# Attention scores of a head pair in two row halves of the array, in six bursts instead of eleven steps

## The chip, the cores and the metric

The kernel runs on one core of one Trainium2 chip. A core has a matmul engine (PE, whose weight loads PEld overlap its matmuls), a vector engine (DVE), a scalar engine (ACT), a general engine (POOL) and a queue engine that issues DMAs (SP). Matmuls write PSUM, eight banks of 512 floats in each of 128 partitions; DVE and ACT read them there, POOL cannot. Each engine works its instructions in order and waits on semaphores that the others raise. The metric is device time in microseconds (us), the median of a few runs. For the kernel before it is 1928.92 us (three runs, 1925.21 to 1930.3).

## The reference

Input x has 2048 tokens of width 576. What is computed, cut to what matters:

```
h   = layernorm(x) * (1 + ca) + sa
q, k, v = h @ wq, h @ wk, h @ wv         # 32 heads of width 18, 4 segments of 512 tokens
p   = softmax(q k^T / sqrt(18) + causal mask)     # inside a segment
a   = g * (phi(q) @ M) / (phi(q) @ z) + (1 - g) * (p @ v)    # M, z: sums over earlier segments
x   = x + ga * (a @ wo)
h   = layernorm(x) * (1 + cb) + sb
out = x + gb * ((silu(h @ w_gate) * (h @ w_up)) @ w_down)
```

## The kernel before, in words

Three stages follow one another. **Projections** (to about 256 us): x is normalized, transposed and multiplied by the projection weights, each product as three matmuls of high and low halves; q, k and v go to DRAM (qD, kD, vD). **Attention** (about 256 to 613 us). **Feed-forward** (the rest).

Attention works in 32 *units*: segment s = 0 to 3 by group q = 0 to 7 of four heads. A unit has two passes over its scores. The *first pass* (`p1_step`, L177) multiplies queries by keys (matmul L187) into PSUM bank s1, and DVE takes each row's maximum (L192, a custom reduction followed by a read of its accumulator). After the last one POOL splits the negated maxima into high and low parts (L197 to L200), PE transposes them (`mt_a`, L206), ACT copies them to mr (L210) and issues their store to DRAM buffer mD (L211); `load_m` (L173, issued by SP) reads them back into two extra rows of the query stack. The *second pass* (`p2_step`, L578) multiplies again (L589), now with those two rows against rows of ones in the key stack, so that the maxima are subtracted by the matmul itself; ACT takes the exponential out of bank s2 into Pt (L592), POOL zeroes the masked corner (L596). Then `av_step` (L600) multiplies by the values: four heads' matmuls of 32 output columns each (L609), one group for each of four key blocks j; these are full float32 and appear as two instructions each, where the score matmuls are rounded float32 and appear as one. `ev_step` copies av out (ACT, L621), `comb_a` transposes it (PE, L630), `comb_b` scales it by the row sums (DVE) and adds it to the memory part (POOL).

The operands of the scores are *stacks*. For a pair of heads the key stack holds 108 rows: head e=0 in rows 0 to 53, head e=1 in rows 54 to 107 (18 dimensions, three times for the high, high and low parts), and the ones in rows 108 and 109. The query stack has four slots, one for each head, and in each slot the rows of the other head of the pair are zero (`new_stack`, L122, writes the zeros by memset). So each head's score matmul uses 108 or 110 of 128 rows, of which 54 carry data. There are four sets of stacks (b = u % 4); `load_stack` (L164) fills one with four DMAs.

In the main loop (L1284 to L1297) a pass over unit u loads the stacks of unit u+3, runs the second pass of unit u and the first pass of unit u+2, and the rest of the neighbours' work. The order is written out by hand (`manual_schedule`): both passes are generators of eleven steps (four steps each for 512 and 384 columns, two for 256, one for 128), one step of each is taken in turn, and after step k come the *events* that the string PAT[..][k] lists. PAT has four rows: q below 4 or not, u even or odd. Both passes rotate through two banks (S1B, S2B = 2), one bank a step.

Events that matter here: V0 to V3 the value matmuls of block j (V2 and V3 belong to the unit before); E, c, d its copy-out, transpose and combination; m and n the transpose of the maxima, and their copy, store and reload; M0 to M3 quarters of an output projection (`wo_m`, PE, L707) and X its addition (DVE); R, S, T the transpose, copy and low part of its input; l, p, x the statistics (DVE), power (POOL) and normalization (`ln_c`, ACT, L739) of the following layernorm; g three ACT activations on queries of the next segment (`phi_q2`, L756 to L758), in the first five units of segments 0 to 2; A0, A1, B0, B1, C, D, G the memory product for the next segment (`num_a` on PE, L778, `num_b` on ACT, L787), in the last four units of segments 0 to 2; P, Q, q, Y the preparation of the output weights, in segment 0; f a DMA.

The first passes of units 0 and 1 (`early`, L256) run among the projections, where a scheduler orders instructions; `p1_unit` (L213) is a generator there.

Of the kernel before, what the change touches and what calls it, by code (L numbers as in the profile page):

```python
# [15 lines left out]
P = 128  # L16
S = 2048
# [44 lines left out]
PAT = (["", "V2", "V3 E m D", "M0", "n M1 Q G", "c", "M2 d", "V0 g", "h A0 q M3 R S X", "T Y Z B0", "A1 P V1 z B1 f C"],  # L62
       ["V2 D", "l M0 Q", "V3 m E", "M1", "G p n A0 B0 M2", "", "M3 X A1 q c x d B1", "f", "V0 g", "", "C V1 Y h P"],
       ["", "V2", "V3 m E", "M0", "D G M1 c n", "", "Q V0 d g R", "h", "M2 q M3 A0 S B0 X", "Z Y", "P f z V1 A1 T B1 C"],
       ["", "V2 m", "l D n p G M0", "V3", "M1 E M2 A0", "", "M3 x c", "B0", "V0 d Q", "A1 g", "q X V1 Y B1 h P C f"])
# [9 lines left out]
def block(ctx: ExitStack, tc: tile.TileContext, x, wqk, wv, wo, beta, wgu, wd, c, w_mod, out):  # L75
# [46 lines left out]
    def new_stack(b, stk):  # L122
        qst[b] = stk.tile([P, 4, L], F32R, tag=f"qs{b}", name=f"qs{b}")
        kst[b] = stk.tile([P, 2, L], F32R, tag=f"ks{b}", name=f"ks{b}")
        nc.vector.memset(f32(qst[b][:, 0:2]), 0.0)
        nc.gpsimd.memset(f32(qst[b][:, 2:4]), 0.0)
        nc.sync.dma_start(f32(kst[b][108:110]).rearrange("p a (b c) -> p (a b) c", c=P),
                          ones[0:2, :].unsqueeze(1).to_broadcast([2, 8, P]))
# [35 lines left out]
    def load_stack(u, b):  # L164
        s, q = units[u]
        for e in range(2):
            v = [d[s].rearrange("f z t -> (f z) t").rearrange("(Q a e r) t -> Q e r a t", Q=8, a=2, e=2)[q, e]
                 for d in (kD, qD)]
            r = slice(54 * e, 54 * e + 54)
            nc.sync.dma_start(f32(kst[b][r]), v[0])  # L170
            nc.sync.dma_start(f32(qst[b][r, e:4:2, :]), v[1])

    def load_m(u, b):  # L173
        nc.sync.dma_start(f32(qst[b][108:110]).rearrange("p a t -> p (a t)"),
                          m_dram(u).rearrange("(a b) t -> a (b t)", a=2))

    def p1_step(u, b, i, ps, jp, jb):  # L177
        if i == 3:
            mcol[u] = (mwk.tile([P, 4, 4], F32, tag="mx", name="mx"),
                       mwk.tile([P, 2, 4, 4], F32R, tag="mc", name="mc"))  # L180
        mx, mc = mcol[u]
        n = 128 * (i + 1)
        per = L // n if n <= 256 else 1
        for h0 in range(0, 4, per):
            bank = ps.tile([P, L], F32, tag="s1", name="s1", bufs=S1B)
            for h in range(h0, h0 + per):
                nc.tensor.matmul(bank[:, n * (h - h0):n * (h - h0) + n],  # L187
                                 lhsT=qst[b][0:108, h, 128 * i:128 * i + 128],
                                 rhs=kst[b][0:108, h // 2, 0:n], start=True, stop=True)
            for h in range(h0, h0 + per):  # L190
                junk = jp.tile([P, L], BF16, tag="junk", name="junk", bufs=jb)
                nc.vector.tensor_tensor_reduce(junk[:, :n], bank[:, n * (h - h0):n * (h - h0) + n], tri[:, L - n:],  # L192
                                               1.0, -3e38, op0=ALU.add, op1=ALU.max, accum_out=mx[:, h, i:i + 1])
            if h0 + per < 4:
                yield
# [5 lines left out]
        yield  # L201
# [11 lines left out]
    def p1_unit(u, b, ps, tag, bufs, jp, jb):  # L213
        for i in range(4):
            yield from p1_step(u, b, 3 - i, ps, jp, jb)
# [355 lines left out]
    def p1_seq(u):  # L571
        if NE <= u < NU:
            for i in range(4):
                yield from p1_step(u, u % NB, 3 - i, ps, wk, 4)

    Pt, av = {}, {}

    def p2_step(u, j):  # L578
        if u >= NU:
            return  # L580
        n = L - 128 * j
        per = L // n if n <= 256 else 1
        pt = pp_.tile([P, 4, n], F32, tag=f"P{j}", name="Pt", bufs=1)
        Pt[u, j] = pt
        for h in range(0, 4, per):
            bank = ps.tile([P, L], F32, tag="s2", name="s2", bufs=S2B)
            for g in range(h, h + per, 2):
# [966 lines left out]
```

## Time and profile before

| what | value |
|---|---|
| median of three runs | 1928.92 us |
| the profiled execution, its own time | 1926.12 us |
| its span (first to last instruction) | 1924.3 us |
| granted clock of PE, mean over the span | 0.996 |
| stage with attention units | about 256 to 613 us |

The profile shows one execution. A row of a group or timeline reads: source line, engine, operation, output <- input, shapes; then busy time or start and duration in us, and in brackets the idle time before it with what ended it. In a merged timeline row the time is that from the first start to the last end. Matmuls overlap, since the next one fills the array while the last one drains: the duration shown for one (about 0.4 us) is longer than the distance to the next (about 0.235 us for 512 columns). In the chain of waits each piece is what the one before it did not cover, so there the distance is shown.

### The profile page before, as it was taken

The page shows a single profiled execution, that of the slowest core. Times are in us where ns is not written, and L with a number is a line of the kernel's source. Part 1 is how long each engine was busy: PE and PEld are TensorE (multiplying, and loading weights), DVE is VectorE, ACT ScalarE, POOL GpSimd, SP SyncE. Part 2 cuts the span into 40 slices and gives each one's busy share as a digit, 9 for nine tenths or more (in the row PEclk, how much of TensorE's full clock was granted, in tenths as well). Part 3 has the DMA queues.
Part 4 walks back from the last instruction along what each step waited for, and adds up shares of the span by engine and source line. Part 5 has one row for each costly group of instructions (what it writes and reads, how often), then busy time and mean ns, then how long its engine had stood idle before and what let it go on. Part 6 is the DMA issues. An engine that isn't in the chain of part 4 may idle for free.

```text
span 1924.3 us, 30622 instructions
## 1 busy us (share of the span) xinstructions
PE 1874.0 (97%) x10927; PEld 1562.5 (81%) x10927; DVE 1512.8 (79%) x3267; ACT 929.8 (48%) x2036; POOL 581.0 (30%) x772
## 2 busy tenths in 40 slices
PE   7999999999999799999999999999999999999999
PEld 4888865676766678888888888888888888888888
DVE  6575257878786888898898888776888888888887
ACT  2222257767666444445445444443544444454542
POOL 5222235555544554545444545410000000000000
PEclk9999999999999899999999999999999999999999
DMA  7777565444443555454454554478333233333331
GB/s 209 251 230 245 199 200 150 124 147 145 138 127 117 172 199 175 155 191 151 159 186 154 163 168 145 137 246 267 101 106 113 79 122 101 122 101 97 106 108 60
DMA packets 173543, 296.63 MB, mean 154 GB/s; under 512 B 25104, under 2 KB 101776, under 8 KB 171920
## 3 DMA queue, kind: packets, MB, share of 16 engines
q1 hardware_dynamic: 143280, 237.09, 39.4%
q10 hardware_dynamic: 30112, 57.60, 8.6%
q8 instruction: 86, 1.41, 0.3%
q14 instruction: 65, 0.53, 0.1%
HBM read 185.29 MB, written 109.31 MB: 153 GB/s over the span
## 4 chain that ended last, share of the span: by engine, by line
PE 88%; DMA 5%; DVE 4%; POOL 1%; issue 1%; ACT 1%; SPq 0%; ACTq 0%; POOLq 0%; DVEq 0%
PE A L1136 23%; PE pd L1257 13%; PE C L1136 12%; PE pd L1240 9%; PE B L1136 6%; PE s L589 4%; PE av L609 4%; PE pp L101 4%; PE s L187 4%; PE pv L101 3%; PE pw L707 2%; DMA y<-yD 1%; DMA mD<-mr 1%; PE pn L778 1%; DVE y L938 1%
## 5 line engine op out<-in xcount | busy, mean ns | idle before, releaser
L1136 PE MATMUL A<-y,wh 128*128 128x512 f32 x1152 | 406.8, 394 | 4.3 <-ACT B L1182 1.8
L192 DVE CUSTOM_DVE_ANT_0 junk<-s,tri 128x256 bf16<-128x256 f32 (+3 forms) x512 | 228.6, 487 | 75.6 <-PE s L187 67.6
L1101 DVE TENSOR_TENSOR wl<-O,wh 128x256 fp32r<-128x256 f32 x504 | 261.7, 525 | 4.2 <-ACT wh L1100 3.5
L1136 PEld LDWEIGHTS A<-y,wh 128*128 128x128 f32 x1152 | 217.2, 189 | 49.0 <-ACT B L1182 2.5
L592 ACT ACTIVATE Pt<-s 128x512 f32<-128x512 f32 (+1 forms) x352 | 186.6, 559 | 86.2 <-PE s L589 71.6
L1136 PE MATMUL A<-y,wl 128*128 128x512 f32 x576 | 227.2, 394 | 0.0
L1091 POOL TENSOR_TENSOR O<-O 128x384 f32<-128x384 f32 x144 | 163.3, 1146 | 179.1 <-DMA O<-in_wgu_dram 76.0
L1245 DVE TENSOR_TENSOR acc<-acc,pd 128x576 f32<-128x576 f32 x216 | 162.4, 752 | 58.6 <-PE pd L1240 51.7
L1136 PE MATMUL C<-y,wh 128*128 128x512 f32 x576 | 202.6, 392 | 1.0 <-DVE cu L1159 1.0
L1100 ACT CAST wh<-O 128x256 fp32r<-128x256 f32 x504 | 196.4, 405 | 1.9 <-POOL dr__8754 L1119 1.2
L1257 PE MATMUL pd<-dh,ah 128*128 128x288 f32 x640 | 189.1, 295 | 0.1
L1257 PE MATMUL pd<-dh,al 128*128 128x288 f32 x640 | 189.1, 295 | 0.0
L1257 PE MATMUL pd<-dl,ah 128*128 128x288 f32 x640 | 188.9, 295 | 0.0
L1261 DVE TENSOR_TENSOR acc<-acc,pd 128x576 f32<-128x576 f32 x156 | 116.9, 749 | 89.0 <-PE pd L1257 88.9
L1200 ACT CAST ah<-sg 128x512 fp32r<-128x512 f32 x192 | 119.1, 620 | 82.7 <-DVE sg L1160 77.6
L589 PE MATMUL s<-qs,ks 110*128 110x512 f32 (+2 forms) x384 | 149.2, 405 | 6.6 <-DMA qs<-mD 4.8
L187 PE MATMUL s<-ks,qs 108*128 108x256 f32 (+3 forms) x512 | 140.7, 326 | 2.9 <-DMA ks<-kD 1.4
L1201 DVE TENSOR_TENSOR al<-sg,ah 128x512 fp32r<-128x512 f32 x192 | 135.2, 704 | 8.8 <-ACT ah L1200 8.4
L1240 PE MATMUL pd<-dh,ah 128*128 128x288 f32 x448 | 133.0, 297 | 0.0
L1240 PE MATMUL pd<-dh,al 128*128 128x288 f32 x448 | 132.5, 296 | 0.0
L1240 PE MATMUL pd<-dl,ah 128*128 128x288 f32 x448 | 132.3, 295 | 0.0
L1257 PEld LDWEIGHTS pd<-dl,ah 128*128 128x128 f32 x640 | 120.5, 188 | 7.1
(349 smaller groups left out, 4394.4 us busy)
## 6 DMA issues: line engine op xcount, KB each, us to landing
O<-in_wgu_dram SPq DMA_DIRECT2D x36, 768.0 KB
oD<-O ACTq DMA_DIRECT2D x36, 512.0 KB
O<-oD SPq DMA_DIRECT2D x36, 512.0 KB
ks<-kD SPq DMA_DIRECT2D x68, 216.0 KB
qs<-qD SPq DMA_DIRECT2D x68, 216.0 KB
O<-in_wgu_dram SPq DMA_DIRECT2D x36, 384.0 KB
rD<-wr ACTq DMA_DIRECT2D x36, 336.0 KB
wr<-rD SPq DMA_DIRECT2D x35, 336.0 KB
```

Of the source, the lines that this page charges most:

```text
L187: nc.tensor.matmul(bank[:, n * (h - h0):n * (h - h0) + n], lhsT=qst[b][0:108, h, 128 * i:128 * i + 128], rhs=kst[b][0:108, h // 2, 0:n], s ...
L192: nc.vector.tensor_tensor_reduce(junk[:, :n], bank[:, n * (h - h0):n * (h - h0) + n], tri[:, L - n:], 1.0, -3e38, op0=ALU.add, op1=ALU.max ...
L589: nc.tensor.matmul(bank[:, n * (g - h):n * (g - h + w)].rearrange("p (a b) -> p a b", a=w), lhsT=kst[u % NB][0:110, g // 2, 128 * j:128 * ...
L592: nc.scalar.activation(pt[:, h:h + per, :n], bank[:, :n * per].rearrange("p (a b) -> p a b", a=per), AF.Exp, scale=SCALE)
L1091: nc.gpsimd.tensor_tensor(o[:, d], o[:, a], o[:, b], op=op)
L1100: nc.scalar.copy(wh, o)
L1101: later.append(lambda: nc.vector.tensor_tensor(wl, o, f32(wh), op=ALU.subtract))
L1136: nc.tensor.matmul(bank, lhsT=a, rhs=b, start=(first and n == 0), stop=(n == 6), skip_group_check=not first)
L1201: later.append(lambda: nc.vector.tensor_tensor(al, src, f32(ah), op=ALU.subtract))
L1240: nc.tensor.matmul(pd[:, i, :288], lhsT=a[:, tk], rhs=w, start=(k == 0), stop=(k == 2))
L1245: nc.vector.tensor_tensor(o, o, pd[:, :, :288], op=ALU.add)
L1257: nc.tensor.matmul(pd[:, i, :288], lhsT=a[:, tk], rhs=w, start=(k == 0), stop=(k == 5))
```

## The change

The two heads of a pair no longer share one column of rows. Key stack and query stack hold head e=0 in rows 0 to 53 and head e=1 in rows 64 to 117; each half has its own two rows of ones (keys) and of maxima (queries) behind its 54. The query stack shrinks from four slots to two, and the zeros with their memsets are gone. Each score matmul reads only the 54 or 56 rows of its half, and the built program gives it a tile of 64 rows by 128 columns at row 0 or 64. The ones are written by two DMAs a stack instead of one, the maxima are read back by two instead of one; the stack loads keep their count and size.

The eleven steps become six bursts (BI gives the row block, BA the pairs): two with 512 columns, two with 384, one with both pairs of 256, one with both pairs of 128. A burst takes both s1 banks, one for each half, and issues the first-pass matmuls in the order e=0, e=1, then its reductions; the second pass does the same with both s2 banks and its exponentials, now two instructions in every burst. The second pass no longer joins two heads in one matmul for the narrow blocks: 16 matmuls a unit instead of 12, and 12 exponentials instead of 11. The events are regrouped into six strings in each row of PAT.

```diff
-PAT = (["", "V2", "V3 E m D", "M0", "n M1 Q G", "c", "M2 d", "V0 g", "h A0 q M3 R S X", "T Y Z B0", "A1 P V1 z B1 f C"],
-       ["V2 D", "l M0 Q", "V3 m E", "M1", "G p n A0 B0 M2", "", "M3 X A1 q c x d B1", "f", "V0 g", "", "C V1 Y h P"],
-       ["", "V2", "V3 m E", "M0", "D G M1 c n", "", "Q V0 d g R", "h", "M2 q M3 A0 S B0 X", "Z Y", "P f z V1 A1 T B1 C"],
-       ["", "V2 m", "l D n p G M0", "V3", "M1 E M2 A0", "", "M3 x c", "B0", "V0 d Q", "A1 g", "q X V1 Y B1 h P C f"])
+PAT = (["V2 M0", "V3 E m D M1", "n Q G c M2", "d V0 g", "h M3 A0 q R S X Y Z B0", "T A1 P V1 z B1 f C"],
+       ["V2 D l M0 Q", "V3 m E M1", "n G p A0 c M2", "d V0 g B0 q x", "M3 A1 X B1 f", "C V1 Y h P"],
+       ["V2 M0", "V3 m E M1", "n D G c M2", "Q V0 d g R", "h M3 q A0 S X Z Y B0", "P f z V1 A1 T B1 C"],
+       ["V2 m l M0", "V3 E n D p G M1", "A0 c M2 x", "B0 V0 d Q", "M3 A1 g X q", "V1 Y B1 h P C f"])
+BI = (3, 3, 2, 2, 1, 0)
+BA = ((0,), (1,), (0,), (1,), (0, 1), (0, 1))
...
-        qst[b] = stk.tile([P, 4, L], F32R, tag=f"qs{b}", name=f"qs{b}")
+        qst[b] = stk.tile([P, 2, L], F32R, tag=f"qs{b}", name=f"qs{b}")
...
-        nc.vector.memset(f32(qst[b][:, 0:2]), 0.0)
-        nc.gpsimd.memset(f32(qst[b][:, 2:4]), 0.0)
-        nc.sync.dma_start(f32(kst[b][108:110]).rearrange("p a (b c) -> p (a b) c", c=P),
-                          ones[0:2, :].unsqueeze(1).to_broadcast([2, 8, P]))
+        for e in range(2):
+            nc.sync.dma_start(f32(kst[b][64 * e + 54:64 * e + 56]).rearrange("p a (b c) -> p (a b) c", c=P),
+                              ones[0:2, :].unsqueeze(1).to_broadcast([2, 8, P]))
...
     def load_m(u, b):
-        nc.sync.dma_start(f32(qst[b][108:110]).rearrange("p a t -> p (a t)"),
-                          m_dram(u).rearrange("(a b) t -> a (b t)", a=2))
+        v = m_dram(u).rearrange("(c a e i) t -> e c a (i t)", c=2, a=2, e=2)
+        for e in range(2):
+            nc.sync.dma_start(f32(qst[b][64 * e + 54:64 * e + 56]), v[e])
...
+        banks = [ps.tile([P, L], F32, tag="s1", name="s1", bufs=S1B) for _ in range(2)]
+        for x, a in enumerate(BA[t]):
+            for e in range(2):
+                r = slice(64 * e, 64 * e + 54)
+                nc.tensor.matmul(banks[e][:, n * x:n * x + n], lhsT=qst[b][r, a, 128 * i:128 * i + 128],
+                                 rhs=kst[b][r, a, 0:n], start=True, stop=True)
+        for e in range(2):
+            for x, a in enumerate(BA[t]):
...
+                nc.vector.tensor_tensor_reduce(junk[:, :n], banks[e][:, n * x:n * x + n], tri[:, L - n:],
...
     def p1_unit(u, b, ps, tag, bufs, jp, jb):
-        for i in range(4):
-            yield from p1_step(u, b, 3 - i, ps, jp, jb)
+        for t in range(6):
+            p1_burst(u, b, t, ps, jp, jb)
+            yield
+            yield
...
+    def p2_burst(u, t):
...
+        banks = [ps.tile([P, L], F32, tag="s2", name="s2", bufs=S2B) for _ in range(2)]
+        w = len(BA[t])
+        for x, a in enumerate(BA[t]):
+            for e in range(2):
+                r = slice(64 * e, 64 * e + 56)
+                nc.tensor.matmul(banks[e][:, n * x:n * x + n], lhsT=kst[u % NB][r, a, 128 * j:128 * j + 128],
+                                 rhs=qst[u % NB][r, a, 128 * j:L], start=True, stop=True)
+        for e in range(2):
+            h = 2 * BA[t][0] + e
+            nc.scalar.activation(pt[:, h:h + 2 * w - 1:2, :n], banks[e][:, :n * w].rearrange("p (a b) -> p a b", a=w),
                                  AF.Exp, scale=SCALE)
...
-            for k in range(11):
-                next(ga, None)
-                next(gb, None)
-                for ev in PAT[q // 4 * 2 + u % 2][k].split():
+            for t in range(6):
+                if NE <= u + 2 < NU:
+                    p1_burst(u + 2, (u + 2) % NB, t, ps, wk, 4)
+                if u < NU:
+                    p2_burst(u, t)
+                for ev in PAT[q // 4 * 2 + u % 2][t].split():
                     event(ev, u)
```

## The prediction

> **What bounds the kernel now.** I read the page first (span and busy shares), then busy time in windows cut at attention units, then the chain of waits inside one unit, then single rows for prices.
>
> ```profile
> span 1924.3 us, 30622 instructions
> PE 1874.0 (97%) x10927; PEld 1562.5 (81%) x10927; DVE 1512.8 (79%) x3267; ACT 929.8 (48%) x2036; POOL 581.0 (30%) x772
> ```
>
> The matmul engine is the pace-maker on average, but the change touches only the attention stage (about 256 to 613 us) and two early units inside the projections, so an average decides nothing. Five units, by window (PE, weight loads, DVE, ACT, POOL):
>
> ```profile
> core 0: us, PE busy (x) PEld busy (x) DVE busy (x) ACT busy (x) POOL busy (x), PEclk, DMA share, GB/s
> 311.00:322.47 11.47, 10.28 (x78) 6.77 (x77) 10.14 (x45) 7.84 (x17) 8.44 (x17) 1.00 0.52 141
> 446.24:457.14 10.90, 10.90 (x83) 7.35 (x79) 10.04 (x44) 8.68 (x18) 4.18 (x10) 1.00 0.49 151
> 457.14:468.28 11.14, 11.14 (x88) 7.70 (x84) 8.46 (x34) 8.73 (x18) 6.71 (x12) 1.00 0.45 135
> 504.13:516.44 12.31, 12.31 (x97) 8.94 (x94) 9.56 (x43) 7.28 (x15) 6.44 (x16) 1.00 0.55 150
> 550.86:562.00 11.14, 11.14 (x88) 7.70 (x84) 8.46 (x34) 7.06 (x14) 3.65 (x9) 1.00 0.42 132
> ```
>
> They are units 5, 17, 18, 22 and 26. PE is never idle in the last four, but DVE needs 8.5 to 10.0 us and ACT 7.1 to 8.7 us of each: whatever PE gives up, at most 1 to 3 us can be kept, and less where a queue is lumpy. The chain inside unit 22 (start, us, work):
>
> ```profile
> 504.87 0.23 PE s L589
> 505.10 0.23 PE s L187
> 505.33 0.57 PE av L609 x8
> 505.90 0.43 PE s L589
> ...
> 506.55 0.36 PE av L609 x8
> ...
> 509.50 0.18 PE s L187
> ...
> 510.02 1.00 PE av L609 x8
> ...
> 512.19 0.24 PE s L187 x2
> 514.09 0.24 PE s L589
> 514.57 0.24 PE s L589 x2
> 514.81 0.40 PE s L187 x4
> ```
>
> A score matmul costs 0.235 us for 512 columns, 0.18 for 384, 0.12 for 256, 0.10 for 128. One unit's first pass (L187: four of each width) is 2.53 us; the second (L589: four of 512, four of 384, two paired to 512, two paired to 256) is 2.37. Together 4.9 us of 12.3.
>
> **Part 1: pairs in two 64-row halves.** The same columns are streamed, but heads e=0 and e=1 stand in different row halves and write different banks. No row of this profile has two row halves in work. The nearest is av, four 32-column tiles: 8 instructions in 0.36 us for 128 columns and 1.00 for 512, so 0.21 us per further 128 columns for eight, where one score matmul takes 0.06 per 128 columns. Eight one after another could not; the four tiles run side by side. So a pair costs between 1.0 and 2.0 single matmuls; I take 1.0. Scores become 1.26 + 1.26 = 2.5 us, PE saves 2.4 us a unit; at 2.0 it saves nothing, and the four 128-wide second-pass matmuls that replace two 256-wide ones cost 4 x 0.10 - 2 x 0.12 = 0.16 more.
>
> The Trainium skill, page "TensorE: Matmul & The Clock Gate", section "Part 3: Packing small matmuls — row/col tiling", gives 3.07 times for four row tiles; scaled to two (an estimate from that figure) a pair costs 1.3 singles, the saving falls to 1.7 us a unit, and a unit bound by PE alone would gain 0.8 instead of 1.5 us. No run here shows it yet.
>
> **Part 2: array modes.** Every burst sets the array to 64-row tiles while av uses 32 columns and all else the whole array. In the built order of the matmuls the changes of tile shape grow from 257 to 432 within attention (5.5 more a unit) and from 34 to 79 before it. The price stands in the rows: after av, a 512-column score matmul takes 0.43 instead of 0.24, so 0.19 to leave; av's 0.36 less its 0.21 per 128 columns leaves 0.15 to enter. A 64-row tile already occurs among the projections, in the last transposes of a key block:
>
> ```profile
> 38.39 0.40 PE L101 MATMUL pp<-hr,wqkl 128*128 128x512 f32 x1
> 38.62 0.60 PE L429 MATMUL ptk<-ident,pf 128*128 128x128 f32 x4
> 39.30 0.40 PE L101 MATMUL pp<-hh,wqkl 128*128 128x512 f32 x1
> 53.19 0.40 PE L101 MATMUL pp<-hr,wqkl 128*128 128x512 f32 x1
> 53.52 0.46 PE L429 MATMUL ptk<-ident,pf 64*128 64x64 f32 x4
> 54.24 0.39 PE L101 MATMUL pp<-hh,wqkl 128*128 128x512 f32 x1
> ```
>
> From the projection before to the second one after: 0.91 us with whole-array transposes, 1.05 with 64-row ones although those are 0.14 shorter: 0.28 for in and out. So a switch is 0.14 to 0.19; I take 0.17. Attention pays 5.5 x 0.17 = 0.9 us a unit.
>
> The skill's page "TensorEngine Tiling (Array Packing)", section "Tiling Modes", says that changing the mode drains the engine, which speaks against short bursts; these rows agree and give the price, 0.17 us.
>
> PE alone would so gain 2.4 - 0.9 = 1.5 us a unit.
>
> **Part 3: what the other engines allow.** A burst fills both banks of each pass, so the next burst needs two reductions and two exponentials done. Before, each of eleven steps took one bank of two.
>
> ```profile
> 452.86 0.87 ACT L739 ACTIVATE xh<-xr,nb,rs 128x576 f32<-128x576 f32 x1
> 453.63 0.96 ACT L592 ACTIVATE Pt<-s 128x384 f32<-128x384 f32 x2
> 454.48 0.63 ACT L756 ACTIVATE qe<-qf 128x512 f32<-128x512 f32 x1
> 455.14 0.63 ACT L757 ACTIVATE qe<-qe 128x512 f32<-128x512 f32 x1
> 455.68 0.61 ACT L758 ACTIVATE qf<-qf 128x512 f32<-128x512 f32 x1
> 456.20 1.06 ACT L592 ACTIVATE Pt<-s 128x512 f32<-128x512 f32 x2
> ```
>
> Odd units of segments 1 and 2 with q below 4 (9, 11, 17, 19): events g and x, two steps apart before with exponentials between, now both stand behind burst 4. I walk PE: four bursts 0.17 + two pairs (0.64, 0.64, 0.53, 0.53), av 0.57 and 0.36, the small transposes and seven projection matmuls about 2.4, 0.35 wait because ln_a now sits on DVE behind burst 1: burst 4 ends at 6.1. Its two exponentials end at 7.05, g (1.8 from start to end) at 8.85, x at 9.7, burst 5's two exponentials (1.06) at 10.8. Burst 6's second pass waits until then (PE was ready near 9.5); with 0.2 for it and about 0.8 for av the unit ends at 11.9, against 10.9 for unit 17. The four together +3.3 us. Their even neighbours have only g there: 10.75 against 11.14 (unit 18); the four of them -1.3.
>
> Full units (segments 1 and 2, q from 4; like unit 22) have pn and pw between the bursts: PE stays the bound, -1.0 after the DVE wait of the odd ones; six of them, -0.6 for unit 20 and 0 for unit 12 (next paragraph): -6.6. Segment 3 (like unit 26) loses its cover: burst 6 waits for burst 5's four reductions (DVE's L192 is 228.6 us over 32 units, 7.1 each, first row below), ending near 10.5: -0.5 a unit, -3.7 for units 24 to 30.
>
> ```profile
> L192 DVE CUSTOM_DVE_ANT_0 junk<-s,tri 128x256 bf16<-128x256 f32 (+3 forms) x512 | 228.6, 487 | 75.6 <-PE s L187 67.6
> 282.32 4.51 DMA mD<-mr
> 280.43 0.34 SPq L171 DMA_DIRECT2D qs<-qD  x1
> 286.84 0.23 SPq L174 DMA_DIRECT2D qs<-mD  x1
> 320.30 2.04 DMA qs<-mD
> ```
>
> Segment 0, and units 11, 12 and 19, wait for the row maxima's way through DRAM: written at 282.32 behind stack loads issued until 280.43, landed only when SP issues the read at 286.84, 2.04 more to land, and the next unit starts. Those loads keep their size, so the units keep their length. The maxima's copy now stands behind six exponentials instead of five, and there are two reads instead of one (0.23 of SP): +0.2 to +0.8 where the loads did not already set it. Segment 0 together +1.4.
>
> Attention: 3.3 - 1.3 - 6.6 - 3.7 + 1.4 = -6.9 us.
>
> **Part 4: outside.** The scheduler spreads the first two units' bursts among projections: 45 more switches, 7.6 us, less some 1.5 for pairs that stay together.
>
> ```profile
> by line: PE pp L101 33.3%; PE pv L101 20.3%; DVE junk L192 5.1%; issue 4.8%; DMA wml<-in_w_mod_dram 4.7%; PE s L187 3.7%; DVE macc L303 3.2%; DVE x L232 3.1%; PE pt L237 2.9%; PE pc L310 2.3%; POOL rs L228 2.0%; DVE pk L433 1.7%; PE ptk L42
> 245.85 1.49 SPq L127 DMA_DIRECT2D ks<-ones  x2
> 250.43 0.76 SPq L171 DMA_DIRECT2D qs<-qD  x1
> 250.43 8.83 DMA qs<-qD
> ```
>
> The first row is the chain from 85 to 160 us, about 63% PE, so 6.1 x 0.63 = +4 (bounds 0 and 7.6). At the stage's start the ones take four issues instead of two ahead of unit 2's loads, whose landing (last row) held unit 0: +1.4 (bounds 0 and 1.5). The removed zeroing (eight memsets) delayed no PE work there; I give it 0.
>
> **Sum**: -6.9 + 4 + 1.4 = -1.5 us. The profiled execution took 1926.12 us (1.8 outside its span), 2.8 below the median of 1928.92; so 1924.6 on its scale, 1927 on the median's.
>
> **Rivals.** (a) *PE keeps what it saves.* For it: PE is 100% busy in four of the five units. Then 24 units (all but the eight held by the maxima) gain 1.5: 1928.9 - 36 + 5.4 = 1898. Against it: DVE already 10.0 in unit 17. (b) *ACT's lump spreads.* All 15 units that carry g, not just four, wait for burst 5's exponentials. It decides once ACT has over about 2.2 us (av 1.00, a burst 0.5, pw 0.7) between the exponentials of bursts 4 and 5; g alone is 1.8. Eleven more at +1.1: 1939. (c) *The change doesn't do what it says*: halves do not overlap. Each unit then pays 0.9 + 0.2: 32 x 1.1 = 35, half of it hidden in the eight held units, so 31, + 5 + 1.4: 1966. For it: each second half waits on a semaphore of its own.
>
> **How the numbers follow.** My forecast, an even trade, 0.45, own range 1918 to 1937; (a) 0.20; (b) 0.20; (c) 0.15. Change smaller than 0.3% (5.8 us) can't be told from none. Of the even trade 0.12 falls faster, 0.20 within, 0.13 slower. Faster 0.12 + 0.20 = 0.32, same 0.20, slower 0.13 + 0.20 + 0.15 = 0.48. The range 1905 to 1958 leaves out half of (a) and two thirds of (c). It includes a pair a third of the way to no overlap (1.3 singles: 0.7 us less on some 13 units that PE bounds, +9) and switches at 0.14 or 0.19 (5 us either way).
>
> **What would show it.** Scores of a pair starting together, at most 0.02 us apart; matmuls after a burst 0.15 to 0.2 late; units 17 and 18 near 11.9 and 10.75, unit 22 near 11.3; the weight-load queue waiting for ACT ahead of burst 6; the projections some 4 us longer. I am wrong if PE still has no idle time in odd units, or if second halves start only when first halves end.

## The result, and the profile after

The change makes the kernel slower: 1975.68 us against 1927.47 (medians of four runs each), ratio 1.0249 with a 95% interval of 1.0231 to 1.0266. The forecast was 1927 in a range of 1905 to 1958; it is wrong.

The span grew by 48.5 us, from 1924.3 to 1972.8. I cut it at the first exponential of a unit (in the trace every 11th row of `Pt<-s` on ACT before, every 12th after):

| part | before | after | difference | forecast |
|---|---|---|---|---|
| start to unit 0's first exponential (projections, start of the stage) | 257.5 | 272.3 | +14.8 | +5.4 |
| from there to unit 31's | 346.3 | 377.3 | +31.0 | -6.9 |
| the rest | 1320.5 | 1323.2 | +2.7 | 0 |

The page of after, its head and the row of the granted clock in 40 slices of 49.3 us:

```profile
span 1972.8 us, 30927 instructions
PE 1904.1 (97%) x11055; PEld 1535.7 (78%) x11055; DVE 1506.8 (76%) x3263; ACT 926.8 (47%) x2068; POOL 573.5 (29%) x768
PEclk9999976999999999999999999999999999999999
```

PE's busy time rose by 30 us although it has less to stream, and the clock shows 0.7 and 0.6 in the slices where attention starts. In windows (columns: busy us and instructions of each engine, granted clock, DMA), cut at the start of attention and behind units 5 and 30, after reads

```profile
240.00:271.50 31.50, 27.01 (x165) 24.29 (x163) 3.91 (x7) 5.54 (x12) 2.48 (x4) 0.97 0.81 263
271.50:349.00 77.50, 71.35 (x414) 34.03 (x416) 49.45 (x211) 49.35 (x106) 35.55 (x56) 0.66 0.43 123
349.00:649.00 300.00, 283.64 (x2179) 162.25 (x2177) 225.14 (x933) 194.93 (x425) 141.50 (x295) 0.96 0.42 121
```

and before, for the same units as the last two,

```profile
256.50:323.00 66.50, 58.82 (x392) 34.61 (x392) 51.55 (x213) 49.67 (x102) 36.90 (x60) 1.00 0.56 164
323.00:603.00 280.00, 279.08 (x2076) 193.42 (x2074) 222.66 (x931) 197.81 (x400) 139.76 (x291) 1.00 0.43 129
```

The clock takes two values, 1.0 and 0.5, in stretches of 3.41 us or a multiple. Summed, 109 us of after ran at half clock up to 740 us (20 before unit 0, 76 in attention, 14 behind it) against 14 of before. The largest wait of PE's two queues in attention (us in all, times, longest), in after and then in before, shows the other change: the weight loads of a burst now wait for DVE's reductions, where those of a step waited, for less, for ACT's exponentials.

```profile
PEld s L190 <- DVE mx L195: 70.0, 152, 1.3
```

```profile
PEld s L589 <- ACT Pt L592: 39.9, 66, 1.4
```

So three suspects: G, the granted clock, set off by thinner streaming; W, waits of the paired bursts for banks and events; M, the mode switches. The Trainium skill, page "TensorE: Matmul & The Clock Gate", section "Part 1: The HAM clock gate (the "warmup" mystery)", describes a gate with two states, full and half, decided over free-running windows of 3413 ns, and warns of idle gaps over about 3.4 us; "A second HAM failure mode: psum-queue depth-cycling" there tells of short idles between groups of matmuls that cycle through banks. The two values and the 3.41-us grid of this trace agree. The forecast had no term for it.

### The profile page after: what moved, and what is told of

It reads as the page before. It is cut to its first block, busy times and chain, and to the rows that moved or that the text cites. A ratio compares the mean times of both kernels' runs of the same rounds, so it can differ in the third digit from the quotient of the medians.

```text
span 1972.8 us, 30927 instructions
## 1 busy us (share of the span) xinstructions
PE 1904.1 (97%) x11055; PEld 1535.7 (78%) x11055; DVE 1506.8 (76%) x3263; ACT 926.8 (47%) x2068; POOL 573.5 (29%) x768
## 4 chain that ended last, share of the span: by engine, by line
PE 83%; DVE 8%; DMA 3%; ACT 2%; POOL 2%; issue 1%; SPq 1%; ACTq 0%; DVEq 0%; POOLq 0%
PE A L1133 22%; PE pd L1254 12%; PE C L1133 11%; PE pd L1237 9%; PE B L1133 6%; PE pp L103 5%; PE s L190 4%; DVE junk L195 3%; PE av L606 3%; PE pv L103 3%; PE pw L704 2%; PE s L587 2%; DMA y<-yD 1%; PE px L627 1%; PE pn L775 1%
## 5 line engine op out<-in xcount | busy, mean ns | idle before, releaser
L591 ACT ACTIVATE Pt<-s 128x512 f32<-128x512 f32 (+2 forms) x384 | 180.8, 523 | 121.5 <-PE s L587 108.3
L190 PE MATMUL s<-ks,qs 54*128 54x256 f32 (+3 forms) x512 | 125.7, 426 | 20.7 <-DVE mx L195 15.5
L190 PEld LDWEIGHTS s<-ks,qs 54*128 54x128 f32 x512 | 61.5, 198 | 106.5 <-DVE mx L195 71.7
L594 POOL TENSOR_SCALAR_AFFINE_SELECT Pt<-Pt 128x512 f32<-128x512 f32 x128 | 81.3, 635 | 186.0 <-ACT Pt L591 186.0
```

The costliest lines, as they stand in the source:

```text
L190: nc.tensor.matmul(banks[e][:, n * x:n * x + n], lhsT=qst[b][r, a, 128 * i:128 * i + 128], rhs=kst[b][r, a, 0:n], start=True, stop=True)
L591: nc.scalar.activation(pt[:, h:h + 2 * w - 1:2, :n], banks[e][:, :n * w].rearrange("p (a b) -> p a b", a=w), AF.Exp, scale=SCALE)
```

## The experiments

**Each part alone.** The first four kernels: the other order in unit 0; bursts without halves; halves without bursts; more streaming.

```diff
@@ e1: main loop, bursts of unit u @@
+                if u == 0:
+                    p2_burst(u, t)
                 if NE <= u + 2 < NU:
                     p1_burst(u + 2, (u + 2) % NB, t, ps, wk, 4)
-                if u < NU:
+                if 0 < u < NU:
                     p2_burst(u, t)
@@ e2: bursts alone (stacks, load_stack, load_m as before) @@
-    lhsT=qst[b][r, a, 128 * i:128 * i + 128], rhs=kst[b][r, a, 0:n]
+    lhsT=qst[b][0:108, 2 * a + e, 128 * i:128 * i + 128], rhs=kst[b][0:108, a, 0:n]
@@ e3: halves alone, in the eleven steps of before @@
-    lhsT=qst[b][0:108, h, 128 * i:128 * i + 128], rhs=kst[b][0:108, h // 2, 0:n]
+    r = slice(64 * (h % 2), 64 * (h % 2) + 54)
+    lhsT=qst[b][r, h // 2, 128 * i:128 * i + 128], rhs=kst[b][r, h // 2, 0:n]
@@ e4: e1, and in the main loop's p1_burst @@
-        for x, a in enumerate(BA[t]):
+        for x, a in [v for v in enumerate(BA[t]) for _ in range(1 + (ps is ps2_[0]))]:
```

> The kernel after, with one difference: in the first burst group of the attention stage (unit 0 alone) the second pass's pairs of unit 0 are issued ahead of the first pass's pairs of unit 2, whose operands the loads bring only 5 us later; every other unit keeps its order. Theory G (the loss of 48 us is the granted TensorE clock: 109 us at half clock after against 14 before, and each such 3.4-us window loses half of itself): TensorE no longer idles at 266 to 271 us, so the 5 us of idle go and with them much of the 41 us at half clock between 270 and 314 us; the time falls by 10 to 25 us, to 1951 to 1966 us, and time at half clock falls to 60 to 80 us. Rival W (the loss is waits of the pairs for banks that VectorE still reads; the lower clock is a trace of that and costs nothing of its own): only the idle goes, 1969 to 1972 us, wherever the clock is.

> The kernel after with the old zero-padded stacks of 108 and 110 rows: the same six bursts in the same order, the same banks, reductions and exponentials, but every score matmul takes the whole height of the array, so no two overlap and the mode of the array changes about as often as in the kernel before (296 runs of one mode in the program, 294 before, 514 after). Theory G: TensorE streams as long as in the kernel before, so the windows stay busy enough and the clock stays up but for the idle at the start of the stage; half-clock time under 50 us and 1930 to 1950 us, faster than the kernel after although each pair costs double. Rival W (bank waits of the bursts): the bursts and their banks are all there, so 1960 us or more with the clock near full. Rival M (the array-mode switches cost the 48 us): they are gone, so about 1930 us, but then the clock does not matter and is about as low as in the kernel after.

> The kernel before with 64-row stacks: eleven steps and their order as before, each score matmul takes one half of the rows, one bank at a time, heads of one half share a bank where two heads share one (so the 128-column step takes two banks and two exponentials instead of one); hardly any two overlap, as the halves that follow each other are mostly the same. The mode changes 558 times against 294 before and 514 after. Theory G: TensorE streams as long as before, the clock stays up; what is left is the price of the switches, at my 0.17 us for 264 more and three quarters of them on the path some 30 us, 1935 to 1960 us with under 30 us at half clock. Rival M (switches cost the 48 us): 1970 us or more. Rival W: the banks go one by one as before, so 1927 to 1935 us.

> The second-pass-first kernel with each pair of the first pass in the attention stage issued twice into the same banks (480 more matmuls, 1.2 us of TensorE a unit at full clock and overlap; the second writes what the first wrote). It is work for nothing, which raises the busy share of the windows. Theory G: less than 40 us at half clock, and the time is no higher than that of the second-pass-first kernel, 1930 to 1955 us. Rival W: each bank is ready 0.24 us later, and VectorE and the exponentials with it; 15 to 37 us above the second-pass-first kernel.

| kernel | median, us | ratio to before, 95% | first exponential | attention | half clock in attention |
|---|---|---|---|---|---|
| after | 1975.68 | 1.0231 to 1.0266 | 272.3 | 377.3 | 76.0 |
| e1, second pass first | 1975.2 | 1.0207 to 1.0270 | 268.2 | 380.7 | 71.7 |
| e2, bursts alone | 1960.2 | 1.0127 to 1.0182 | 266.9 | 372.0 | 20.5 |
| e3, halves alone | 2029.3 | 1.0477 to 1.0566 | 266.4 | 445.2 | 170.7 |
| e4, pairs twice | 2001.9 | 1.0350 to 1.0402 | 267.8 | 410.1 | 68.3 |

No theory came through whole. e1 only moved the wait for unit 2's loads into unit 0 (15.8 us long instead of 12.5) and the clock dropped at 271 us all the same. e2 did lower the time at half clock as G said, by 55 us, but gained only 15 us, 5 of them in attention; as it also streams longer, it does not price the clock by itself. In e3, where PE streams as long as before but in single halves, the clock was worst, which G as I had put it did not allow. In e4 half as much score work again (the first pass twice) changed the half-clock time by 3 us, against G, and cost 27, as W had it.

Units that never see half clock tell the rest without it. In the eight full ones (13 to 16 and 21 to 24), summed: before 95.5 us, after 93.1, e2 97.7, e3 104.4. So at full clock bursts cost 0.27 us a unit, halves in bursts give back 0.57, and halves without bursts cost 1.12, for 220 more mode changes in 32 units: 0.16 us each, a little less if the four more second-pass matmuls a unit are taken off.

**Where events stand.** In after, units 11, 17, 19, 25 and 27 are 1.2 to 4.1 us longer than before. Unit 25, first ACT, then POOL, then PE:

```profile
583.98 0.87 ACT L591 ACTIVATE Pt<-s 128x384 f32<-128x384 f32 x2 [0.61 <-PE s L587]
587.24 0.87 ACT L736 ACTIVATE xh<-xr,nb,rs 128x576 f32<-128x576 f32 x1 [2.39 <-POOL nb L735]
588.02 1.06 ACT L591 ACTIVATE Pt<-s 128x512 f32<-128x512 f32 x2
```

```profile
586.17 0.79 POOL L644 TENSOR_TENSOR o<-o,tmp 128x288 f32<-128x288 f32 x1 [0.60 <-DVE tmp L643]
586.95 0.26 POOL L735 TENSOR_SCALAR nb<-mv,rs 128x1 f32<-128x1 f32 x1
```

```profile
586.08 0.29 PE L704 MATMUL pw<-wol,or 128*128 128x288 f32 x1
...
588.65 0.32 PE L587 MATMUL s<-qs,ks 56*128 56x128 f32 x1 [0.70 <-ACT Pt L591]
```

ACT stands 2.39 us at xh: its operand nb is queued on POOL behind comb's add (event d), which waits for DVE. The exponentials of burst 5 wait behind xh, and PE's last burst for their banks. In the list of before, x stood ahead of d. The next four kernels move x, and fill the idle at the start of the stage.

```diff
@@ e5: PAT, odd units, q below 4 (e8: the same edit on e2) @@
-"d V0 g B0 q x"
+"x d V0 g B0 q"
@@ e6: e5 and e1, and in p1_burst for unit 2, first burst @@
-            for e in range(2):
+            for e in [0] * (10 * (u == NE and t == 0)) + [0, 1]:
@@ e7: PAT of before @@
-"M3 X A1 q c x d B1"
+"M3 X A1 q c d x B1"
```

> The kernel after with one event moved inside one list: in the odd units of the first half of a segment, x (POOL's nb, then ScalarE's normalised row xh) is issued ahead of d instead of behind q. In the trace of after ScalarE stands 2.4 us in unit 25 at xh, because nb waits on POOL behind d's add, which waits for VectorE; the exponentials of the 256-column burst are queued behind xh, and TensorE's last burst waits for their banks. Units 11, 17, 19, 25 and 27 are the ones with x in this list; they are 1.9, 3.9, 1.2, 2.7 and 2.3 us longer than before, and half-clock windows follow 11, 17 and 25. Theory L (the place of x makes the lumps, and the lumps trigger those drops): those units shrink by 1 to 2.5 us each, 7 to 12 us together, and the 24 us at half clock behind them go, worth 4 to 8 us; 1956 to 1965 us. Rival (the lumps come from the bursts themselves, whatever event stands there): 1972 to 1976 us.

> The x-ahead kernel with the second pass of unit 0 first (as in the second-pass-first kernel), and ten extra copies of the first score matmul of unit 2, written to the bank that it writes anyway, in the 2.2 us in which TensorE waits for the other half of that unit's loads: work for nothing in an idle that is there anyhow. Theory G: the window that was 0.20 busy rises to 0.75 or more, the drop at 271 us does not come, half-clock time in units 0 to 5 falls from about 53 us to under 25, and the time is 5 to 12 us below the x-ahead kernel. Rival (the clock does not go by how much TensorE streams): the drops stay where they were, and the time is 0 to 3 us above it.

> The kernel before, with x put behind d in the same list (odd units, first half of a segment), nothing else changed: the reverse of the x-ahead edit. Theory L in its strong form (the order of x and d alone makes the lump): units 11, 17, 19, 25 and 27 grow by 1 to 2.5 us each, 1933 to 1940 us. In its weak form (the order costs only where a whole burst's exponentials queue behind xh; in eleven steps one exponential at a time is late and the next step covers it): 1927 to 1931 us.

> The bursts-alone kernel (full-height matmuls, no row halves) with x ahead of d. Theory L: units 17, 25 and 27 are 2.1, 3.2 and 1.6 us above before in the bursts-alone kernel and give 1 to 2 us each, 11 and 19 some 0.8 each; 1952 to 1957 us against 1960. What it stands above the kernel before is then the bursts' own price (about 0.3 us a unit at full clock, 9 us) and the projections' and the start's (10 us). Against the x-ahead kernel it tells what the row halves bring in the same schedule: by the full-clock units 14, 16, 22 and 24 about 0.7 us a unit less with halves, 10 to 20 us in all, if the clock is the same in both; if the halves lower the clock, the two come out within 8 us of each other.

| kernel | median, us | ratio to before, 95% | attention | units 11, 17, 19, 25, 27 | half clock in attention |
|---|---|---|---|---|---|
| before, its profiled run | | | 346.3 | 10.9, 10.8, 11.6, 10.8, 10.9 | 0 |
| after | 1975.68 | 1.0231 to 1.0266 | 377.3 | 12.8, 15.0, 12.8, 13.8, 13.2 | 76.0 |
| e5 | 1969.4 | 1.0193 to 1.0239 | 377.3 | 13.6, 14.3, 13.1, 13.4, 11.8 | 77.3 |
| e6 | 1972.1 | 1.0212 to 1.0253 | 379.4 | 13.3, 13.9, 14.5, 12.2, 11.8 | 75.1 |
| e7 | 1941.8 | 1.0060 to 1.0102 | 361.4 | 13.5, 13.1, 13.4, 13.7, 12.6 | 17.1 |
| e8 | 1961.4 | 1.0157 to 1.0210 | 373.8 | 14.5, 13.8, 13.6, 12.1, 11.6 | 20.5 |

Of the forecasts, that of e7 came nearest (2 us above the range of L's strong form); e5 stands between its two and e8 above its own. e6 came out as its rival said, 2.7 us above e5.

e7 settles the order of x and d: swapping the two letters in the kernel before, and nothing else, costs 15.1 us, with the same stall in its ACT row:

```profile
559.69 0.87 ACT L739 ACTIVATE xh<-xr,nb,rs 128x576 f32<-128x576 f32 x1 [2.63 <-POOL nb L738]
```

In e5 and e6 the swap back took most of the lump out of unit 27 and, in e6, of unit 25, which have no g; they still stand 0.9 and 1.3 us above before. In 11, 17 and 19, which have g as well, another lump remained (in e8 these three even grew by 0.8 to 2.0 us over e2 and took back what 25 and 27 gave), the one of my prediction's Part 3: in e6's unit 17 xh and g's three operations keep ACT from 486.11 to 488.67 between two bursts' exponentials.

```profile
486.11 0.87 ACT L736 ACTIVATE xh<-xr,nb,rs 128x576 f32<-128x576 f32 x1 [1.00 <-POOL nb L735]
486.88 0.61 ACT L753 ACTIVATE qe<-qf 128x512 f32<-128x512 f32 x1
487.52 0.63 ACT L754 ACTIVATE qe<-qe 128x512 f32<-128x512 f32 x1
488.06 0.61 ACT L755 ACTIVATE qf<-qf 128x512 f32<-128x512 f32 x1
488.58 1.06 ACT L591 ACTIVATE Pt<-s 128x512 f32<-128x512 f32 x2
```

And filling the wait at the start did not hold the clock: the window from 269.5 us was streaming for 0.51 of its length, nearly all of it single half-height matmuls, and the clock dropped behind it.

**The edits together, and the rows.**

```diff
@@ e9: after, e12: e2, both with @@
-E1 = 3
+E1 = 4
...
-    def new_stack(b, stk):
+    def new_stack(b, stk, ahead=None):
...
+        if ahead and b == 2:
+            ahead(2)
...
         for b in range(2, NB):
-            new_stack(b, sk2)
+            new_stack(b, sk2, load_unit)
         for j in range(4):
             load_v(0, j)
-        load_unit(2)
...
-       ["V2 D l M0 Q", "V3 m E M1", "n G p A0 c M2", "d V0 g B0 q x", "M3 A1 X B1 f", "C V1 Y h P"],
+       ["V2 D l M0 Q", "V3 m E M1", "n G p A0 c x M2", "d V0 i B0 q", "M3 A1 j X B1 f", "k C V1 Y h P"],
...
+            if n == "k":
+                nc.scalar.activation(f[r:], f[r:], AF.Relu)
+            else:
+                nc.scalar.activation(e[r:], (f if n == "i" else e)[r:], AF.Relu if n == "i" else AF.Exp, scale=-1.0)
@@ e10: e6, with this ahead of unit 2's first burst in place of the ten copies @@
+            for _ in range(3):
+                nc.tensor.matmul(banks[0], lhsT=ident, rhs=tri, start=True, stop=True)
```

> The kernel after with its bursts and row halves as they are, and four edits around them, each read in its own part of the trace. (1) The two early units are advanced four steps a projection instead of three, which makes the scheduler put VectorE's splits hl ahead of the modulation sums macc that wait for a load; the 4.0-us wait of TensorE for hl at 159 us and the half-clock windows at 133 and 160 us should go: projections end at 254 to 260 us instead of 266. (2) Unit 2's operands are loaded ahead of the ones and the values: the idle of 5 us at the start of the stage and the drop behind it should go; units 0 to 3 together 44 to 48 us instead of 51. (3) In the odd units of the first half of a segment x is issued one burst earlier, and (4) ScalarE's three operations of g are spread over three bursts. Theory L2 (the lumps of units 11, 17 and 19 are xh and g, 2.7 us of ScalarE in a row between two bursts' exponentials): these units come to 11 to 12.5 us from 12.8 to 15.0, and the drops behind them go. Theory G as a whole: time at half clock falls from 109 us to under 50, and the time to 1930 to 1948 us, about an even trade with the kernel before. Rival (bursts and halves themselves cost, wherever events stand): 1960 us or more.

> The combined kernel with full-height matmuls in place of row halves (the bursts-alone kernel with the same four edits). By the full-clock units the halves are worth 0.4 to 0.9 us in the even units and 0.4 in the odd ones, 10 to 18 us over the stage, so 1940 to 1960 us if the clock is alike in both; if theory G also tells the halves from the full height (less streaming, so more drops with halves), this kernel has less time at half clock than the combined one and stands within 8 us of it.

> The filled-start kernel with three full-height fp32 matmuls of 512 columns in the wait at the start of the stage in place of ten copies of a half-height one (which left that window 0.51 busy, and the clock dropped all the same). Theory G with rows (a half-height matmul counts about half in what the clock goes by): the drop at 273 us does not come or comes over 10 us later, and the time is 3 to 8 us under that kernel's 1972 us. Theory G without rows (only the busy time of the window counts): as in that kernel, within 3 us of it, as the window is filled about as much.

| kernel | median, us | ratio to before, 95% | first exponential | attention | half clock in attention |
|---|---|---|---|---|---|
| e9, combined | 1955.8 | 1.0114 to 1.0171 | 263.8 | 367.7 | 54.6 |
| e12, the same at full height | 1945.3 | 1.0057 to 1.0118 | 257.7 | 366.6 | 13.7 |
| e10, full-height fill | 1970.5 | 1.0188 to 1.0241 | 269.6 | 379.8 | 78.5 |

e9 missed its range by 8 us, with 73 us at half clock in all where under 50 was forecast, but most of its edits did what each was to do: the projections' wait is gone, that for unit 2's loads too, unit 17 fell from 15.0 to 11.8 us, unit 25 to 11.8, unit 27 to 11.1; unit 19 hardly moved (12.8, then 12.7). Units 0 and 1 got longer (15.3 and 13.0 against 12.5 and 12.4). That wait in the projections, in after: the scheduler had put DVE's sum macc, which waits for a load, ahead of the split hl that PE needs.

```profile
161.26 0.82 DVE L306 SCALAR_TENSOR_TENSOR macc<-wml,sg,macc 96x576 f32<-96x576 f32 x1 [4.00 <-DMA wml<-in_w_mod_dram]
162.00 1.28 DVE L84 TENSOR_TENSOR hl<-hf,hh 128x512 fp32r<-128x512 f32 x2
```

```profile
162.73 0.79 PE L103 MATMUL pp<-hl,wqkh 128*128 128x512 f32 x1 [3.98 <-DVE hl L84]
```

e9 against e12 is the row halves alone, in one schedule. Until the first exponential they cost 6.1 us: the early units' score matmuls lie among the projections there, with 42 more mode changes (76 against 34) and the same 3.4 us at half clock, so 0.15 us each if all of it is theirs. In attention the halves save streaming; two bursts of unit 22, e9 and then e12 (start, us, work; x2 is one pair, x4 two):

```profile
532.55 0.56 PE L192 MATMUL s<-ks,qs 54*128 54x512 f32 x2
532.89 0.45 PE L589 MATMUL s<-qs,ks 56*128 56x512 f32 x2
533.27 0.43 PE L608 MATMUL av<-Pt,vq 128*32 128x128 f32 x8
...
538.12 0.50 PE L192 MATMUL s<-ks,qs 54*128 54x256 f32 x4
538.46 0.40 PE L589 MATMUL s<-qs,ks 56*128 56x256 f32 x4
538.79 0.40 PE L706 MATMUL pw<-wol,oh 128*128 128x288 f32 x1
```

```profile
521.26 0.64 PE L191 MATMUL s<-ks,qs 108*128 108x512 f32 x2
521.74 0.63 PE L587 MATMUL s<-qs,ks 110*128 110x512 f32 x2
522.30 0.43 PE L606 MATMUL av<-Pt,vq 128*32 128x128 f32 x8
...
527.05 0.72 PE L191 MATMUL s<-ks,qs 108*128 108x256 f32 x4
527.61 0.65 PE L587 MATMUL s<-qs,ks 110*128 110x256 f32 x4
528.09 0.29 PE L704 MATMUL pw<-wol,oh 128*128 128x288 f32 x1
```

From a burst's first matmul to what follows it is 0.72 us against 1.04, and 0.67 against 1.04. Unit 22 takes 11.62 us against 12.54, the eight full units 93.4 against 97.6. Yet the whole stage is 1.1 us longer with halves: 41 us more at half clock, some 12 by the price below, took most of the gain back. By the medians e12 is 10 us faster than e9.

e10 says little: its filling lies ahead of 272 us, and the window from there (0.44 streaming, most of it half height) lost the clock. Its time, 1.7 us under e6, is the one forecast for a gate that does not weigh rows.

**Waste work.** What was left is whether the low clock is cause or company in units 0 to 8.

```diff
@@ e11, e13: e9, units 0 to 8, behind p2_burst(u, t); fill is the bank of tag "w" @@
+ e11:  for _ in range(3):
+           nc.tensor.matmul(fill, lhsT=kst[u % NB][0:54, 0, 0:128], rhs=qst[u % NB][0:54, 0, :], start=True, stop=True)
+ e13:  nc.tensor.matmul(fill[:, :384], lhsT=ident, rhs=tri[:, :384], start=True, stop=True)
```

> The combined kernel with waste work: in units 0 to 8, behind each burst of the second pass, three more half-height score matmuls of 512 columns into the bank that the output projection uses only from unit 9 on. They change no mode of the array, no other engine reads them, and TensorE, which waits there for banks and loads, streams 0.65 us more a burst, 3.8 us a unit. Units 0 to 8 of the combined kernel take 109.9 us together, 44.5 of them at half clock. Theory G without rows (the clock goes by the busy time of the window alone): windows of 0.28 to 0.47 rise by about 0.19 and stay up; under 20 us at half clock, 102 to 107 us for these units, 3 to 8 us less in all although more is done. Theory G with rows (a half-height matmul counts about half): drops remain, 20 to 40 us at half clock, 107 to 112 us. Rival (the clock is no cause): 3.8 us a unit of work, a good half of it on the path, 115 us or more.

> The same with one full-height fp32 matmul of 384 columns a burst, identity by the mask (about 0.65 us of streaming too), with two switches of the array's mode each, 12 more a unit at 0.15 us. Theory G in both forms: windows rise and the clock stays up, under 20 us at half clock; units 0 to 8 take 104 to 110 us, the switches giving back part of it. If this one keeps the clock up and the half-height fill does not, rows count. Rival (the clock is no cause): 118 us or more.

| units 2 to 8 | us | of them at half clock |
|---|---|---|
| before | 75.5 | 0 |
| e9 | 81.7 | 23.1 |
| e11, three half-height matmuls a burst | 89.4 | 0 |
| e13, one full-height matmul a burst | 92.2 | 0 |

Windows of e9, e11 and e13 up to 362 us, those of e11 and e13 from where the clock is back at full:

```profile
292.00:362.00 70.00, 64.48 (x446) 32.38 (x450) 50.47 (x214) 46.60 (x103) 37.53 (x66) 0.83 0.45 124
```

```profile
293.00:362.00 69.00, 67.51 (x504) 38.95 (x502) 48.59 (x201) 44.87 (x97) 35.69 (x63) 1.00 0.41 116
```

```profile
284.00:362.00 78.00, 77.32 (x509) 36.32 (x508) 52.94 (x216) 49.29 (x107) 36.27 (x64) 1.00 0.41 113
```

In the traced executions the clock does what G says: with waste work it stays up from unit 2 to 8 in both kernels. In e13 all four executions have a granted clock of 0.990 to 0.992. In e11 the traced one is the fastest of four (0.989); the others have 0.984, 0.976 and 0.971, so filling at half height did not always hold the clock, and where it was lost there is open. The time does not do what G says: units 2 to 8 get 7.7 and 10.5 us longer, units 0 to 8 take 121.7 and 120.7 us, in the range of the rival, and the kernels take 1980.1 us (ratio 1.0244 to 1.0315) and 1965.6 (1.0166 to 1.0201). So e13, and e9 against e12, show that the low clock comes of thin streaming. That filling costs more than the clock did follows only from the price below.

**The price of a microsecond at half clock.** Six kernels share these bursts and halves: after, e1, e5, e6, e9 and e10. In units 1 to 8, 10, 12, 18, 20, 26 and 28 (no x), I set a unit's length less its mean over the six against its half-clock time less its mean: 0.29 us for each us, standard error 0.01 over 84 points, 0.25 in units 1 to 5 and 0.39 in the last five of the list. The Trainium skill, page "TensorE: Matmul & The Clock Gate", section "HAM oscillation — how this bites in real kernels", reckons half of the throttled time. Here it is less, probably because PE has waits in these units that a slower array fills.

The executions of one and the same kernel agree: e11's four have spans of 1963.7, 1974.6, 1982.3 and 1988.4 us, and by their granted clocks some 43, 63, 95 and 115 us at half clock, so 0.33 us for each. Both prices are associations. No kernel here changed the clock and nothing else.

## Why the prediction was wrong, point by point

| share of the 48.5 us | us | from |
|---|---|---|
| switches among the projections | +6.1 | e9 against e12 |
| scheduler's order there, idle at the start, the drops around both | +8.5 | first exponential, after against e9 |
| half clock in attention | +22 | estimate: 76.0 x 0.29 |
| lumps of units 11, 17, 19, 25, 27 | +11 | 12.4 longer, less 1.5 for their 5.1 us at half clock |
| all other units of attention | -2 | remainder; the eight full units alone are -2.4 |
| e12 against before, first exponential | +0.2 | 257.7 against 257.5 |
| behind attention | +2.7 | its half clock is 14 us against 10 |

The steps are the Parts of the prediction.

*Step 1, pairs (1.0 singles).* Right where both banks are free. The halves then start 3 to 4 ns apart, and in e9's burst at 538 us the two pairs of 256 start 0.120 us apart, a single's price. Where a bank is not free they start up to 0.26 apart (542.129 and 542.395 in after). In after's second passes 46% of 248 pairs start at most 0.02 us apart, the sign that I had named, and a quarter 0.12 us or more. So rival (c) is dead, though the full overlap is not the rule.

*Step 2, switches (0.17 us, 0.9 a unit).* Price right: 0.15 and 0.16 measured. But PE alone was to gain 1.5 us a unit, and unit 22 shows 0.92 (e9 against e12). Rival (a) falls with the full units of the next step.

*Step 3, full units (-1.0 each).* Mis-sized: the six that were meant (13 to 15 and 21 to 23) came to -0.22 each, the eight above to -0.30. The even ones gain 0.4 to 0.8 (unit 22 0.43, in e9 0.76), the odd ones nothing: in units 15 and 23 the weight loads wait 2.4 and 1.8 us for DVE's reductions, in 14 and 22 0.5 and 0.3. Bursts alone cost 0.27. Unit 12, put at 0, lost 2.4, with 6.8 us at half clock.

*Step 3, the lump (+3.3).* The mechanism was right; the places were only in part right and the size was not. I saw g and x on ACT in units 9, 11, 17 and 19, but gave units 25 and 27, which have x alone, a gain of 0.5. What I missed is that x also waits on POOL behind d. Unit 17 was put at 11.9 and came to 15.0, unit 18 at 10.75 and came to 13.3, of which 5.8 at half clock. Rival (b), the lump in all units with g, had the right sign and the wrong units.

*Step 3, segment 0 (+1.4) and segment 3 (-0.5 a unit).* Segment 0 came to +12.9, of which its 52 us at half clock are 15 at the price above: by that price it would have been some 2 us shorter than before at full clock (worked out, not shown). In segment 3, unit 24 gained 0.5 as forecast, 28 gained 0.2, and 29 and 30 lost 0.5 and 1.0.

*Step 4, projections (+4).* The switches came to 6.1, my full 6.1 before I took 63% of it: the chain's share of PE there was no reason to discount work that PE does in order. Missing was the scheduler's new order of DVE (4.0 us of wait in one row), which I had not read from the built program.

*Step 4, start of the stage (+1.4).* The ones' issues grew by about what I had put, from 1.49 to 2.77 us of SP ahead of unit 2's loads. What I had missed is PE's order: the burst of unit 2 now stands ahead of unit 0's second pass, which came first before, and waits for those loads for 4.5 us, against 1.9 before:

```profile
266.10 0.29 PE L103 MATMUL pv<-wvl,hr 128*128 128x288 f32 x1
268.73 0.47 PE L190 MATMUL s<-ks,qs 54*128 54x512 f32 x1 [2.33 <-DMA qs<-qD]
271.35 0.76 PE L190 MATMUL s<-ks,qs 54*128 54x512 f32 x1 [2.16 <-DMA qs<-qD]
```

*The step that failed* is the missing one: the sum held no term for the granted clock. Halving the time in which scores stream thins PE's windows: in one schedule attention has 54.6 us at half clock with halves and 13.7 without (e9, e12). In after, units 0 to 5, which PE does not bound, spent 52 of their 77 us at half clock. By the price above this one term is 22 us in attention, nearly half of the loss (an estimate), and the drops set off by the stalls above are in it. The rest of the miss is in the terms above: the lumps, and the projections and the start. An even trade would have needed all of them to go well; e12, with the clock nearly whole and the orders mended, still stands 15 us above before: its attention is 20.3 us longer, 9.7 of them in units 0 to 7, and the clock explains 4 (13.7 us at 0.29).

Open: what the rest in those first units is; the runs do not separate the loads at the start from the coarser steps. No version beat the kernel before.

## What to carry to other kernels

Before shortening the time in which matmuls stream, look at how full the clock's windows are in the stages that the matmul engine does not bound: there the saving buys little, and a fuller engine may be what keeps the clock up. When steps are regrouped, read each in-order queue for what now stands ahead of an operand that another engine waits for; two letters in an event list were worth 15 us here. A mode switch has a price per change, so count changes, and count them in full where the engine works in order.

## What the runs showed of the hardware

For each 3.41-us window at full clock I took the time in which TensorE streams (columns times cycle, from the matmul rows). In the 15 traces, with the first and the last stretch of each kernel left out (25 more drops lie there), 121 of 7,733 such windows are followed by half clock. With all streaming counted alike, the best single threshold (0.41) misplaces 24 windows; with a half-height matmul that runs alone counted half, and a pair counted 0.9, the best threshold is 0.40 and misplaces 14. So the gate seems to weigh rows as well as time, which would explain e3, whose long stay at half clock is the worst of all, and e6's window of 0.51. That is a fit with weights chosen for it, not an experiment: e10, meant to test it, did not, and in their traces e11 and e13 both kept the clock, though by the mean only e13 did so in every execution.

The Trainium skill, page "TensorE: Matmul & The Clock Gate", section "HAM oscillation — how this bites in real kernels", gives the rule that there be no idle gaps over about 3.4 us. Here the windows that lost the clock were streaming for 0.34 of their length in the median, and the longest pause in them was 1.2 us in the median and over 3 us in 6 of the 121. To come back took more: of the windows that ended a stretch at half clock, nine in ten were streaming for 0.79 of their length or more.
